# Chunk attention with two gated feed-forward layers on one Trainium2 core: when block 0's v, the first weights and block 1's q and k are issued

## The chip, the cores and the metric

One core of a Trainium2 chip runs the whole program in one launch. The metric is device time in microseconds (us), lower is better. The kernel before takes 1098.87 us (median of 3 runs, 1097.88 to 1102.31).

## What is computed

```python
B, H, S, D = q.shape                        # 4, 8, 768, 64
chunk, left_ctx, right_ctx = (32, 16, 8)
for c in range(S // chunk):
    k_ctx = k[:, :, l_start:r_end]          # 16 tokens left, 32 own, 8 right
    k_full = np.concatenate([mem_k, k_ctx], axis=2)   # 8 memory keys ahead
    v_full = np.concatenate([mem_v, v_ctx], axis=2)
    scores = scale * np.matmul(q_c, k_full.transpose(0, 1, 3, 2))
    scores = scores - np.max(scores, axis=-1, keepdims=True)
    a = np.exp(scores)
    a = a / (np.sum(a, axis=-1, keepdims=True) + 1e-09)
    out[:, :, c_start:c_end] = np.matmul(a, v_full)
x = out.transpose(0, 2, 1, 3).reshape(B * S, H * D)    # 3072 x 512
h = x @ w_in                                           # 512 x 2048
sp = np.where(h > 20.0, h, np.log1p(np.exp(np.minimum(h, 20.0))))
x = (h * np.tanh(sp)) @ w_out                          # first layer
h = x @ w2_in
return (h * (1.0 / (1.0 + np.exp(-1.702 * h)))) @ w2_out   # second layer
```

q, k, v and the memory are float32, the four weights float64.

## The kernel before, in words

The 3072 tokens are worked in 8 blocks of 384 (TB), two to a batch entry. For each block the attention of its 8 heads comes first, then the first product of layer 1 in 16 chunks of 128 columns (`forward(j, f)`, line 1151, run for f = 0 to 15): chunk f of block 0 is called f0 to f15 here. Block 0 multiplies in plain float32, all later blocks in three products of split values. The attention of block j + 1 is spread among the chunks of block j. Everything behind layer 1's first product is the same before and after and takes no part here.

**Block 0's attention** has 4 pairs of heads, each cut in two: 8 quads (`quad` and `quad_out`, lines 832 and 912). `first_pair` (line 760) loads q and k of a pair in one transfer each (192 KB and 208 KB, k of the first pair 200 KB; they are called q0 to q3 and k0 to k3), q from ACT and k from SP, and PE turns them (line 780). A quad then goes through scores on PE (line 848), masked minima on DVE (862), four exps on ACT (877), reciprocals and scaling (824 to 904, on DVE or ACT), turning on PE (923), a copy to SBUF (929, 930), the product with v (940) and a copy to x (975, 977). `first_memory` (line 739) loads block 0's memory keys and turns them (747). `first_values` (line 723) loads block 0's v for all heads from POOL: four transfers of 208 or 240 KB and four of 16 KB of memory values. A copy of one element on POOL (line 1115) reads the last of the four large ones; POOL's transfers of block 1's v stand behind that copy.

**Weights.** `w_conv` (line 403) loads a chunk of the first weight as float64 words, 512 KB from SP (these loads are W0 to W15), and turns the words to float32 in four steps: a scaled copy on ACT (line 423) or DVE, then a shift, an or and a sign on DVE (432, 436, 440). W8 to W15 go to tiles that hold block 0's raw and turned q and k until then. A conversion is paced by `begun`: the load of chunk f waits for the start of an earlier conversion (AHEAD = 6 back).

**Block 1's attention** goes in pairs of pairs (`pair_of_heads` and `duo`, lines 647 and 991): q and k of a pair come in 4 transfers each of 48 and 52 KB, with 128 bytes in a row, from SP; DVE turns them (679, 682). A duo's scores are 96 small products on PE (line 1003). The first duo's 16 transfers and the second duo's 16 stand on SP with W2 to W7 between them, and W8 follows the second.

**What sets the order.** Each operation is handed to a planner (`Plan`, line 135) with a rank, an engine and a cost; the planner sorts them into one order for each engine before the program is built, and each engine runs its list in that order. An engine that waits holds back all that stands behind it, also the issue of transfers. SP's transfers use 8 semaphores in turn (shared with ACT's), POOL's another 8: a transfer waits for the landing of the one eight before it.

Of the kernel before, what the change touches and what calls it, by code (L numbers as in the profile page):

```python
# [9 lines left out]
F32 = mybir.dt.float32  # L10
# [300 lines left out]
def kernel(  # L311
# [65 lines left out]
    def load(rank, buf, parts, nbytes, run, reads=(), via=0, on=None):  # L377

        for part in parts:
            def go(queue, part=part):  # L380
                o, i = part()
                queue.dma_start(out=o, in_=i)  # L382

            way = ("sp", 0.475, lambda go=go: go(nc.sync), bus(nbytes / len(parts), run))
            if via:
                way = ("pool", via, lambda go=go: go(nc.gpsimd), bus(nbytes / len(parts), run, True))
            if on == "act":
                way = ("act", 0.5, lambda go=go: go(nc.scalar), bus(nbytes / len(parts), run))
            add(rank, [way], reads=reads, writes=[buf])
# [3 lines left out]

    w_src = {
# [8 lines left out]
    def w_conv(layer, f, part, rank, after, v, st):  # L403
# [3 lines left out]
        pace_by = begun[-1 - AHEAD:-AHEAD] if (layer, part) == (1, 0) else [pace[rank - AHEADW]] if rank < L1 else []  # L407
# [195 lines left out]
    x0, mem_t, pace, started, opened = {}, {}, {}, [], []  # L603
# [43 lines left out]
    def pair_of_heads(j, hp, rank):  # L647
# [29 lines left out]
        load(rank - (LEAD if j == 1 and hp < 2 else 4), ql, qs, P * TB * 4, 128, passed(j, rank - AHEADK), via=NARROW * (j > 1))  # L677
        load(rank - (LEAD if j == 1 and hp < 2 else 4), kl, ks, P * NKB * 128, 128, passed(j, rank - AHEADK))
# [19 lines left out]
    def values_of(j, h0, rank):  # L698
# [21 lines left out]
        load(rank, vt, parts, P * NCH * D * 4, 256, opened if j == 1 else passed(j, rank - AHEADV), via=NARROW)  # L720
        return vt

    def first_values(gp, rank):
# [3 lines left out]
        for i in range(2):  # L727
            g = 2 * gp + i
            n0 = LEFT * (g == 0)
            load(rank, vt, [lambda i=i, g=g, n0=n0: (  # L730
                vt[n0:WIN, i], rows(v, g * GQ - LEFT + n0, [(1, WIN - n0), (S, H)], 0, D)
            )], WIN * H * D * 4, 256, via=WIDE)
        for i in range(2):
            load(rank + 0.1, vt, [lambda i=i: (
                vt[WIN:P, i], rows(mem_v, 0, [(1, NM), (NM, H)], 0, D)
            )], 0.05 * WIN * H * D * 4, 256, via=NARROW)
# [23 lines left out]
    def first_pair(hp, rank):  # L760
# [11 lines left out]
        )], 2 * TB * D * 4, 1024, on="act")  # L772
        load(rank - 4, kl, [lambda: (
# [311 lines left out]
    def quads():  # L1085

        last, todo = None, []
        for j in range(NB):
# [17 lines left out]
            for n in range(NQ):  # L1106
                rank = base + 2 * n
                if j == 0:
                    hp, gp = divmod(n, GB // 2)
                    if n == 0:  # L1110
                        first_memory(base - 6)
                        junk = sb.tile([P, 1], F32, name="junk")
# [5 lines left out]
                    if gp == 0:  # L1118
                        qT, kT, done = first_pair(hp, rank)
# [551 lines left out]
```

## Time and profile before

| | |
|---|---|
| median of 3 runs | 1098.87 us |
| the profiled execution | 1095.65 us |
| its span in the profile | 1093.9 us |
| PE, DVE, ACT, POOL busy | 98%, 73%, 49%, 15% of the span |
| DMA moved | 220.83 MB, 202 GB/s on average |
| granted clock of PE, mean of the span | 0.99 |

The profile is of one execution. The page gives busy times and costly groups for the whole span; windows, timelines and the DMA view give a stretch of it, with times in us from the start of the span. A timeline row merges like instructions that follow one another, and the bracket behind it gives the idle time of the engine ahead of it and what ended it. Each of PE's float32 products stands as two records. The granted clock is 1.00 at 2.4 GHz and 0.50 at 1.2 GHz.

### The profile page before, as it was taken

Reading aid. Unit: us, or ns where it says so; the run is one execution under the profiler, and the core shown is the slowest. Engines: PE = TensorE matmul, PEld = TensorE weight load, DVE = VectorE, ACT = ScalarE, POOL = GpSimd, SP = SyncE. Lnnn points to the kernel's source line nnn. Section 1 sums busy time; section 2 is a strip of 40 time slices with the busy share of each in tenths; the row PEclk is TensorE's granted clock in tenths of the full one; section 3 lists DMA queues with packets and bytes.
Section 4 is the critical chain, followed back from the end, with each engine's and each line's share of the span. In section 5 each row is a group of like instructions: output and inputs, shape, how many; then the busy total and the mean of one; then the engine's idle time right before and its main releaser. Section 6 shows DMA issues by size and latency. Waiting matters only on the chain.

```text
span 1093.9 us, 25367 instructions
## 1 busy us (share of the span) xinstructions
PE 1075.9 (98%) x9936; PEld 1039.9 (95%) x9936; DVE 799.5 (73%) x1430; ACT 539.3 (49%) x1209; POOL 163.9 (15%) x273
## 2 busy tenths in 40 slices
PE   6899999999999999999999999999999999999998
PEld 5568999999999999999999999999999999999998
DVE  4896566766677689889869867666657877877875
ACT  4763544544545354555454656565565533323332
POOL 5339347537500000000000000000000000000000
PEclk8799999999999999999999999999999999999999
DMA  9998989989988573573453776868678545355361
GB/s 182 225 249 214 256 256 265 211 244 275 251 268 277 182 233 117 181 245 123 160 173 100 223 251 226 297 216 291 217 256 268 155 121 160 107 146 139 103 167 46
DMA packets 238800, 220.83 MB, mean 202 GB/s; under 512 B 70105, under 2 KB 211997, under 8 KB 238681
## 3 DMA queue, kind: packets, MB, share of 16 engines
q1 hardware_dynamic: 227865, 202.22, 62.6%
q0 software_dynamic: 9984, 16.21, 6.8%
q8 instruction: 78, 1.28, 0.5%
q10 hardware_dynamic: 832, 0.79, 0.3%
q14 instruction: 41, 0.34, 0.1%
HBM read 137.85 MB, written 81.26 MB: 200 GB/s over the span
## 4 chain that ended last, share of the span: by engine, by line
PE 90%; DMA 5%; DVE 4%; issue 1%; ACT 0%; SPq 0%; DVEq 0%; ACTq 0%
PE o L1166 12%; PE h L1166 12%; PE h L1328 9%; PE o L1429 9%; PE o L1521 9%; PE o L1328 8%; PE h L1429 6%; PE s L1429 6%; PE h L1521 6%; PE s L1521 5%; PE s L1328 4%; PE s L1065 1%; DMA wo<-in_q_dram 1%; DMA wi<-in_moe_w_in_dram 1%; PE s L1003 1%
## 5 line engine op out<-in xcount | busy, mean ns | idle before, releaser
L1166 PE MATMUL h<-xh,wi 128*128 128x384 f32 x320 | 83.7, 343 | 0.0
L1166 PE MATMUL o<-xh,wi 128*128 128x384 f32 x320 | 82.8, 340 | 0.0
L1166 PEld LDWEIGHTS o<-xh,wi 128*128 128x128 f32 x320 | 57.1, 188 | 0.6
L1166 PEld LDWEIGHTS h<-xh,wi 128*128 128x128 f32 x320 | 56.9, 188 | 0.6
L1166 PE MATMUL h<-xl,wi 128*128 128x384 f32 x160 | 53.9, 337 | 0.0
L1166 PE MATMUL o<-xl,wi 128*128 128x384 f32 x160 | 53.8, 336 | 0.0
L382 POOL DMA_DIRECT2D vt<-in_v_dram x62 | 41.0, 666 | 30.8 <-PE o L940 14.0
L1298 ACT ACTIVATE e<-h 128x384 f32<-128x384 f32 (+2 forms) x47 | 22.4, 477 | 45.5 <-PE h L1521 28.5
L1511 DVE TENSOR_TENSOR xl<-vt,xh 128x1024 fp32r<-128x1024 f32 x24 | 29.4, 1223 | 20.1 <-ACT xh L1508 18.0
L1521 PE MATMUL o<-wo,xh 128*128 128x256 f32 x232 | 43.7, 282 | 0.0
L1511 DVE TENSOR_TENSOR xl<-wi,xh 128x1024 fp32r<-128x1024 f32 x32 | 38.8, 1221 | 6.6 <-ACT xh L1508 5.9
L1429 PE MATMUL o<-xh,wo 128*128 128x256 f32 x224 | 40.7, 282 | 0.0
L382 POOL DMA_DIRECT2D wo<-in_q_dram x48 | 30.4, 639 | 45.7 <-DMA g1d<-z 16.9
L382 POOL DMA_DIRECT2D wo<-in_v_dram x56 | 35.9, 646 | 5.4 <-DMA wo<-in_q_dram 2.1
L1412 DVE TENSOR_TENSOR xl<-z,xh 128x1024 fp32r<-128x1024 f32 x24 | 29.2, 1223 | 10.2 <-ACT xh L1408 9.4
L1166 PE MATMUL h<-wo,wi 128*128 128x384 f32 x192 | 36.2, 341 | 0.0
L1521 PEld LDWEIGHTS o<-wo,xh 128*128 128x128 f32 x232 | 35.8, 190 | 0.0
L1166 PE MATMUL o<-wo,wi 128*128 128x384 f32 x192 | 35.8, 340 | 0.0
L1508 ACT ACTIVATE xh<-wi 128x1024 fp32r<-128x1024 f32 x25 | 26.4, 1054 | 18.5 <-DMA wi<-gd 8.9
L1298 ACT ACTIVATE ev<-o 128x384 f32<-128x384 f32 (+2 forms) x31 | 14.6, 471 | 42.1 <-PE o L1521 17.9
L1429 PEld LDWEIGHTS o<-xh,wo 128*128 128x128 f32 x224 | 34.8, 191 | 0.0
L1025 ACT ACTIVATE e<-s,mx 128x64 f32<-128x64 f32 x84 | 25.1, 319 | 18.1 <-DVE mx L1020 18.1
(442 smaller groups left out, 3538.8 us busy)
## 6 DMA issues: line engine op xcount, KB each, us to landing
st<-in_moe_w_out_dram SPq DMA_DIRECT2D x32, 512.0 KB
st<-wd SPq DMA_DIRECT2D x29, 512.0 KB
z<-g1d SPq DMA_DIRECT2D x24, 512.0 KB
vt<-gd SPq DMA_DIRECT2D x24, 512.0 KB
wi<-gd SPq DMA_DIRECT2D x24, 512.0 KB
g1d<-gl SPq DMA_DIRECT2D x46, 192.0 KB
g1d<-z SPq DMA_DIRECT2D x45, 192.0 KB
wi<-in_moe_w_in_dram SPq DMA_DIRECT2D x16, 512.0 KB
```

The source lines that it names most:

```text
L382: queue.dma_start(out=o, in_=i)
L1003: nc.tensor.matmul(out=s[hh][c0:c0 + CHUNK, g, i], lhsT=qT[d, c * CHUNK:(c + 1) * CHUNK], rhs=keys[d, c * BLK:c * BLK + KEYS], start=True, ...
L1025: nc.scalar.activation(out=e[:, g, i], in_=s[hh][:, g, i], func=AF.Exp, scale=scale, bias=mx[:, g, i:i + 1], accum_out=sm[:, g, i:i + 1],)
L1065: nc.tensor.matmul(out=o[i][hh * D:(hh + 1) * D, cs], lhsT=vt[hh][d, c], rhs=aT[hh][d, cs], start=True, stop=True, tile_position=(i * D, h ...
L1166: nc.tensor.matmul(out=h.get(), lhsT=a[:, c], rhs=b.at(kk), start=(n == 0), stop=(n == KD * len(prods) - 1))
L1298: ("act", act(n, True), lambda: nc.scalar.activation(out=dst(), in_=bank.get(), func=AF.Copy)),
L1328: nc.tensor.matmul(out=bank.get(), lhsT=a, rhs=b, start=(fresh and m == 0), stop=(m == 3 * K2 - 1), skip_group_check=not fresh,)
L1412: add(rank + 0.05, [("dve", dve(n2), lambda gh=gh, gl=gl, src=src: nc.vector.tensor_tensor(out=flat(gl), in0=flat(src), in1=flat(gh), op=A ...
L1429: nc.tensor.matmul(out=bank[:, d, :], lhsT=a, rhs=b[:, p, :], start=(fresh and h == d == p == m == 0), stop=(h == 1 and p == HP - 1 and m ...
L1508: ("act", act(NP * P), lambda: nc.scalar.activation(out=flat(gh), in_=flat(src), func=AF.Copy)),
L1511: add(rank + 0.05, [("dve", dve(NP * P), lambda: nc.vector.tensor_tensor(out=flat(gl), in0=flat(src), in1=flat(gh), op=ALU.subtract))], re ...
L1521: nc.tensor.matmul(out=bank.get(), lhsT=a[:, p], rhs=b, start=(fresh and p == 0 and m == 0), stop=(p == NP - 1 and m == 2), skip_group_che ...
```

## The change

- POOL's transfers of block 0's v wait for k0: a new copy of one element on POOL reads k0, and v stands behind it.
- SP issues k0 first and the memory keys second.
- A new transfer of 4 bytes on SP, from the last of block 0's large v transfers to a tile `mark`, waits for that v. W0 and all that follows on SP (W1 to W15, block 1's q and k, stores) stands behind its issue; that it has landed is not waited for by W0.
- Block 1's v on POOL still stands behind the copy that reads the last large v.
- The planner's cost for block 0's v changes (the last argument of `bus`), and it sorts the lists of PE, ACT and DVE anew up to the end of block 0's chunks; from there the lists are the same.

```diff
@@ load
-                way = ("pool", via, lambda go=go: go(nc.gpsimd), bus(nbytes / len(parts), run, True))
+                way = ("pool", via, lambda go=go: go(nc.gpsimd), bus(nbytes / len(parts), run, rank > -12))
@@ ahead of w_conv
+    behind = []
@@ w_conv
-        pace_by = begun[-1 - AHEAD:-AHEAD] if (layer, part) == (1, 0) else [pace[rank - AHEADW]] if rank < L1 else []
+        pace_by = begun[-1 - AHEAD:-AHEAD] or behind if (layer, part) == (1, 0) else [pace[rank - AHEADW]] if rank < L1 else []
@@ pair_of_heads
-        load(rank - (LEAD if j == 1 and hp < 2 else 4), ql, qs, P * TB * 4, 128, passed(j, rank - AHEADK), via=NARROW * (j > 1))
-        load(rank - (LEAD if j == 1 and hp < 2 else 4), kl, ks, P * NKB * 128, 128, passed(j, rank - AHEADK))
+        load(rank - (LEAD if j == 1 and hp < 2 else 4), ql, qs, P * TB * 4, 128, behind if j == 1 else passed(j, rank - AHEADK), via=NARROW * (j > 1))
+        load(rank - (LEAD if j == 1 and hp < 2 else 4), kl, ks, P * NKB * 128, 128, behind if j == 1 else passed(j, rank - AHEADK))
@@ values_of
-        load(rank, vt, parts, P * NCH * D * 4, 256, opened if j == 1 else passed(j, rank - AHEADV), via=NARROW)
+        load(rank, vt, parts, P * NCH * D * 4, 256, opened[1:2] if j == 1 else passed(j, rank - AHEADV), via=NARROW)
@@ first_values
-            )], WIN * H * D * 4, 256, via=WIDE)
+            )], WIN * H * D * 4, 256, opened[:1], via=WIDE)
...
-            )], 0.05 * WIN * H * D * 4, 256, via=NARROW)
+            )], 0.05 * WIN * H * D * 4, 256, opened[:1], via=NARROW)
@@ first_pair
+        given.append((ql, kl))
@@ quads
-                        first_memory(base - 6)
-                        junk = sb.tile([P, 1], F32, name="junk")
+                        first_memory(base - 3.95)
+                        junk, mark = (sb.tile([P, 1], F32, name=x) for x in ("junk", "mark"))
+                        qT, kT, done = first_pair(0, rank)
+                        opened.append(fixed())
+                        add(base - 2, [("pool", 0.15, lambda: nc.gpsimd.tensor_copy(
+                            out=junk[32:33], in_=given[0][1][32:33, 0, 0, :1]
+                        ))], reads=[given[0][1]], writes=[opened[-1]])
                         vals0 = [first_values(i, base - 1 + 0.2 * i) for i in range(2)]
...
+                        behind.append(fixed())
+                        add(base + 0.5, [("sp", 0.475, lambda: nc.sync.dma_start(
+                            out=mark[:1], in_=vals0[1][:1, 1, 0, :1]
+                        ))], reads=[vals0[1]], writes=[behind[-1]])
-                    if gp == 0:
+                    elif gp == 0:
                         qT, kT, done = first_pair(hp, rank)
```

Where instructions moved, the lists of the two programs read as follows; what stands in brackets is the semaphore that an instruction waits for (DMAHW for transfers of SP and ACT, DMASW for POOL's).

SP, from its first transfer, before: `w` takes the memory keys, `wi_89` to `wi_113` k0 to k3, `wi_118` and `wi_120` W0 and W1, `wo_123` block 1's first q.

```order
L382 DMA w<-in_mem_k_dram 64x64
L382 DMA wi_89<-in_k_dram 100x2x256
L382 DMA wi_91<-in_k_dram 104x2x256
L382 DMA wi_109<-in_k_dram 104x2x256
L382 DMA wi_113<-in_k_dram 104x2x256 [waits DMAHW0_49]
L382 DMA wi_118<-in_moe_w_in_dram 128x4x256 [waits DMAHW1_49]
L382 DMA wi_120<-in_moe_w_in_dram 128x4x256 [waits DMAHW2_49]
L382 DMA wo_123<-in_q_dram 32x12x32 [waits DMAHW3_49]
```

SP in the changed kernel (`wi_88` is k0, `wi_336` and `wi_347` are W0 and W1):

```order
L382 DMA wi_88<-in_k_dram 100x2x256
L382 DMA w<-in_mem_k_dram 64x64
L382 DMA wi_91<-in_k_dram 104x2x256
L382 DMA wi_110<-in_k_dram 104x2x256
L382 DMA wi_113<-in_k_dram 104x2x256 [waits DMAHW0_49]
L1126 DMA mark<-vt 1x1 [waits DMAHW1_49,DMASW5_49]
L382 DMA wi_336<-in_moe_w_in_dram 128x4x256 [waits DMAHW2_49]
L382 DMA wi_347<-in_moe_w_in_dram 128x4x256 [waits DMAHW3_49]
L382 DMA wo_362<-in_q_dram 32x12x32 [waits DMAHW4_49]
```

k0 and the memory keys have changed places, and `mark`, which waits for POOL's sixth transfer, the last large v, stands ahead of W0.

ACT behind the exps of quad 0, before: the exps of quad 1 (`ev`), then the conversion of W0.

```order
L877 ACTIVATE ev,sm<-ev,mx 96x128 [waits DVE_49] x2
L877 ACTIVATE ev,sm<-ev,mx 96x128
L877 ACTIVATE ev,sm<-ev,mx 96x128 [waits DVE_49]
L423 ACTIVATE wo_291<-wi_118 128x512 [waits DMAHW1_49]
L877 ACTIVATE e,sm<-e,mx 96x128 [waits DVE_49] x2
L877 ACTIVATE e,sm<-e,mx 96x128
L877 ACTIVATE e,sm<-e,mx 96x128 [waits DVE_49]
L929 ACTIVATE z_325<-o_318 128x384 [waits PE_49]
```

ACT from the same place in the changed kernel; `wi_155` takes the turned k of pair 3 and `xh` the first part of x.

```order
L879 ACTIVATE ev,sm<-ev,mx 96x128 [waits DVE_49] x2
L879 ACTIVATE ev,sm<-ev,mx 96x128
L879 ACTIVATE ev,sm<-ev,mx 96x128 [waits DVE_49]
L906 ACTIVATE e<-e,r 96x128 [waits DVE_49,Activation_49]
L906 ACTIVATE e<-e,r 96x128 [waits Activation_49] x3
L879 ACTIVATE e,sm<-e,mx 96x128
L879 ACTIVATE e,sm<-e,mx 96x128 [waits DVE_49]
...
L879 ACTIVATE ev,sm<-ev,mx 96x128 [waits DVE_49]
L808 ACTIVATE wi_155<-h 128x120 [waits DVE_49,PE_49]
L808 ACTIVATE wi_155<-h 128x120
L977 ACTIVATE xh<-o_326 128x192 [waits PE_49]
```

The conversion of W0 is no longer on ACT, where the exps of quad 2 stood behind it; a scaling of quad 0 stands in its place. Between these rows and f0 ACT has no conversion; two splits of W0 and W1 stand among the last quads.

PE at f0, before (`wo_422` and `wo_505` are the turned k of block 1's first duo; 96 scores run from the third row here):

```order
L923 MATMUL o_525<-ident,ev 128x96 [waits DVE_49,PE_49]
L923 MATMUL o_525<-ident,ev 128x96 x3
L1003 MATMUL s_534<-wo_422 32x64 [waits Pool_49]
L1003 MATMUL o_536<-wo_422 32x64
...
L1003 MATMUL o_536<-wo_505 32x64
L940 MATMUL o_593<-z_325,vt 64x96 [waits DVE_49]
...
L940 MATMUL o_662<-z_325,vt 64x96 [waits DVE_49]
L940 MATMUL o_662<-z_325,vt 64x96 x3
L1166 MATMUL h<-xh,wo_291 128x384 x3
L1166 MATMUL h<-xh,wo_291 128x384 [waits DVE_49]
```

PE at the same place in the changed kernel (`wo_527` and `wo_577` are the turned k, `wo_480` holds W0 and W1):

```order
L942 MATMUL o_583<-z_303,vt 64x96 [waits Activation_49]
L942 MATMUL o_583<-z_303,vt 64x96 x3
L1177 MATMUL h<-xh,wo_480 128x384 x3
L1177 MATMUL h<-xh,wo_480 128x384 [waits Activation_49]
L1005 MATMUL s_617<-wo_527 32x64 [waits DVE_49]
L1005 MATMUL o_619<-wo_527 32x64
...
L1005 MATMUL o_619<-wo_577 32x64
L1177 MATMUL h<-xh,wo_480 128x384 x4
L1177 MATMUL o_701<-xh,wo_609 128x384 [waits DVE_49,PE_49]
```

The duo's 96 scores, which stood ahead of the products with v of the last three quads, now stand between f0 (the first two rows of line 1177) and f1 (the last but one).

## Rows read from the trace of the kernel before

**Rows 1.** The page's first part: TensorE's busy time, share, instructions.

```profile
PE 1075.9 (98%) x9936; PEld 1039.9 (95%) x9936; DVE 799.5 (73%) x1430; ACT 539.3 (49%) x1209; POOL 163.9 (15%) x273
```

**Rows 2.** Windows: busy us (count) of PE, PEld, DVE, ACT, POOL; clock, DMA share, GB/s.

```profile
10.00:42.00 32.00, 22.81 (x337) 17.76 (x334) 24.56 (x123) 24.14 (x106) 9.54 (x17) 0.73 1.13 218
40.00:45.00 5.00, 4.35 (x17) 2.61 (x16) 4.55 (x15) 5.00 (x27) 4.75 (x8) 0.50 1.11 151
42.00:54.00 12.00, 12.00 (x38) 7.14 (x37) 9.46 (x23) 7.11 (x23) 8.09 (x16) 0.86 1.19 171
54.00:72.00 18.00, 17.30 (x239) 10.67 (x238) 17.52 (x40) 12.18 (x40) 3.64 (x6) 1.00 1.04 279
```

**Rows 3.** Timeline of PE: start us, us, engine, line, operation, tiles, count, [idle before, releaser].

```profile
22.14 0.91 PE L940 MATMUL o<-z,vt 128*64 128x96 f32 x8 [4.16 <-POOL wo L686]
...
34.80 0.24 PE L1003 MATMUL s<-wo 64*32 64x64 f32 x1
...
36.22 0.91 PE L940 MATMUL o<-z,vt 128*64 128x96 f32 x8
...
42.00 4.47 PE L1166 MATMUL h<-xh,wo 128*128 128x384 f32 x8
...
46.63 2.75 PE L1166 MATMUL h<-xh,wo 128*128 128x384 f32 x8
...
71.56 0.52 PE L1045 MATMUL s<-ident,e 128*128 128x128 f32 x3 [0.70 <-DVE e L1037]
```

**Rows 4.** Timeline of POOL: block 0's v, and the copy that waits for it.

```profile
2.19 2.08 POOL L382 DMA_DIRECT2D vt<-in_v_dram  x2
...
5.39 1.85 POOL L382 DMA_DIRECT2D vt<-in_v_dram  x2
...
18.01 0.18 POOL L1115 COPY junk<-vt 1x1 f32<-1x1 f32 x1 [9.63 <-DMA vt<-in_v_dram]
```

**Rows 5.** Timeline of ACT, 11 to 29 us and at 55 us.

```profile
11.04 0.40 ACT L877 ACTIVATE e<-e,mx 96x128 f32<-96x128 f32 x1 [0.74 <-DVE mx L862]
...
19.46 0.66 ACT L423 ACTIVATE wo<-wi 128x512 f32<-128x512 f32 x1 [5.20 <-DMA wi<-in_moe_w_in_dram]
20.03 0.39 ACT L877 ACTIVATE e<-e,mx 96x128 f32<-96x128 f32 x1
...
21.56 0.47 ACT L929 ACTIVATE z<-o 128x384 f32<-128x384 f32 x1
...
25.70 1.28 ACT L904 ACTIVATE ev<-ev,r 96x128 f32<-96x128 f32 x4 [1.05 <-DVE r L827]
...
28.63 0.33 ACT L975 ACTIVATE xh<-o 128x192 f32<-128x192 f32 x1 [0.87 <-PE o L940]
...
55.26 0.70 ACT L423 ACTIVATE wo<-wi 128x512 f32<-128x512 f32 x1 [3.21 <-DMA wi<-in_moe_w_in_dram]
```

**Rows 6.** Timeline of SP's queue: issues of W and of block 1's q.

```profile
3.97 2.98 SPq L382 DMA_DIRECT2D wi<-in_moe_w_in_dram  x2
6.99 11.70 SPq L382 DMA_DIRECT2D wo<-in_q_dram  x4
...
28.56 5.68 SPq L382 DMA_DIRECT2D wi<-in_moe_w_in_dram  x6
...
48.84 6.51 SPq L382 DMA_DIRECT2D wi<-in_moe_w_in_dram  x6
```

**Rows 7.** DMA view, 0 to 18 us, last row 18 to 34: KB, median us to landing.

```profile
DMA packets 3185, 3.42 MB, mean 190 GB/s; under 512 B 632, under 2 KB 2920, under 8 KB 3184
...
vt<-in_v_dram POOLq DMA_DIRECT2D x3, 240.0 KB, 10.7
...
wo<-in_v_dram POOLq DMA_DIRECT2D x4, 96.0 KB, 5.7
```

**Rows 8.** Timeline of DVE at block 1's last k.

```profile
54.00 0.61 DVE L682 STREAM_TRANSPOSE wo<-z 128x416 f32<-128x416 f32 x1 [1.69 <-DMA z<-in_k_dram]
...
56.48 1.28 DVE L440 SCALAR_TENSOR_TENSOR wo<-wi,wo 128x512 int32<-128x512 int32 x2
```

More of the change, by code (lines that the diff above doesn't have):

```diff
@@ L601, in rows @@
         )
-    x0, mem_t, pace, started, opened = {}, {}, {}, [], []
+    x0, mem_t, pace, started, opened, given = {}, {}, {}, [], [], []
     class Inputs:
```

## The prediction

> **What bounds the kernel now.** First the busy time by engine: TensorE (PE) is busy for 1075.9 of 1093.9 us [rows 1], so at most 18 us of idling and some slow clock can be won. The windows say where it lies. From 10 to 42 us PE is busy for 22.81 of 32 us at a mean granted clock of 0.73; from 42 to 54 it is busy throughout; from 54 to 72 it lacks 0.70 [rows 2]. From there it does not stop, so the prize is the date at which the chunk products f0 to f15 of block 0 begin: 42.00 us [rows 3].
>
> The PE timeline shows the gap ahead of it: the values product of quad 0 starts at 22.14 after 4.16 us of idling [rows 3]. v is not the whole cause. The last of its four large transfers is there at 18.01 [rows 4], but the ACT timeline shows the other one: after the exps of quads 0 and 1, ACT's next instruction is the conversion of W0, for which it waits 5.20 us, until 19.46; the exps of quad 2 stand behind it (20.03) and the copy that feeds the first values product behind those (21.56) [rows 5]. W0 was issued in the stretch that starts at 3.97 [rows 6]: it was in flight for some 15 us, beside q, k and v.
>
> **The change part by part.** *v and W.* In the first 18 us 3.42 MB moved [rows 7]. Block 0 needs 4x192 + 200 + 3x208 KB of q and k, 208 + 3x240 of v, 64 of memory values and 16 of memory keys, 2600 KB or 2.66 MB (the shapes of the transfers). The other 0.76 MB was W and block 1's q. Held back, at 3.42 MB in some 16 us of moving (0.21 MB/us), they give 3.6 us: v at 14.4. Against that v starts later: k0 now goes first on SP, 0.65 us sooner, without memory keys ahead and v beside it. In the trace it was there at about 6.5, when SP's second W was let through (3.97 + 2.98 less its own issue) [rows 6]; I take 5.6. POOL needs 4.1 us from the first to the fourth large v (2.19 to 5.39 + half of 1.85) [rows 4], and v then lands between 5.7 us (the smaller v of block 1) and 10.7 us (v in the crowd) after its issue [rows 7]: 15.4 to 20.4. I take 15.4, nearest to the lower row since the crowd is what is taken away.
>
> *The front, to f0.* ACT no longer meets W0: DVE converts W0 and W1 after the last quads' minima. ACT's list from the first exp to the last copy that f0 needs is 8 quads of 4 exps at 1.53 (20.03 to 21.56), 3 scalings at 1.28, one pair of small copies of k (0.4, about a copy of x), 7 copies of x at 0.33, 5 copies of turned weights at 0.47 and 2 splits of W, for which the nearest row is a conversion at 0.66 [rows 5]: 12.2 + 3.8 + 0.4 + 2.3 + 2.4 + 1.3 = 22.4 us. The first exp began at 11.04 [rows 5]; with k0 earlier, 10.5. Without a pause ACT is done at 32.9. In the trace it also paused for 1.05 and 0.87 us beside the W wait [rows 5]: 34.9 with those. The worst end is all of its idling from 10 to 42 (32 less 24.14 = 7.9 us [rows 2]): 40.8. I take **34.9, so f0 starts 7.1 us sooner** (1.2 to 9.1). DVE, busy for 24.56 of those 32 us [rows 2], has room for the same move. v at 15.4 costs nothing here: by ACT's list the first copy of x comes at 10.5 + 4x1.53 + 1.28 + 0.43 = 18.3, and the values product is wanted just ahead of that. This cover is gone if v lands after about 18.
>
> *Moved behind f0.* The scores of block 1's first duo, 96 small products from 34.80 to 36.22 [rows 3], stand after f0 now: **+1.4 us** once PE is full.
>
> *The hole behind v.* SP waits with mark, W0, W1, 16 transfers of block 1's q and k, W2 to W7, the second 16 and W8 queued behind it. In the trace the first 16 are through when W2 is issued, at 28.56, and W8 goes at 48.84 [rows 6]; ACT gets W8 at 55.26 after a wait of 3.21 [rows 5]. After the change the 16 start at about 17 instead of 6.99, but there they spent 11.70 us on four issues [rows 6], caught behind W, k and v. As 12 of them took 28.56 - 18.69 = 9.9 us, 16 take 13 us: they end at 30, 1.5 us later than before. So W8 comes at 56.8, and f8 can start after ACT's conversion (0.7) and three operations on DVE of up to 0.64 [rows 8], some 3 us with what is queued between them: 60.5. Before, f8 is what PE ends at 70.86, ahead of the 0.70 of idling; at 2.75 us like f1 [rows 3] it began at 68.1, and 5.7 us sooner is 62.4. Covered, with 2 us to spare: **0**. On this wait the Trainium skill has a rule: "DMA: Bandwidth & Descriptors", section "Anatomy of one DMA — SWDGE (gpsimd) path", gives each transfer about 2.0 us of fixed cost, most of it the receipt of the last write, so a queue that is started on a landing stands dry that long. By that page W8 would be at 57.3 and the sum unchanged; no row here shows a dry queue, since the DMA share is 1.13 over those 32 us [rows 2].
>
> *The 4-byte transfer, the memory keys second, POOL's small copy.* SP's mark is one more issue, about 0.5 us, inside the 1.5. Memory keys behind k0 are first wanted when PE's warm-up ends; at worst they delay what I took for k0 by 0.5 us. POOL's copy is 0.18 us [rows 4]. All under cover: 0.
>
> **Sum:** -7.1 + 1.4 = **-5.7 us**. Against the profiled execution, 1095.65 us, that is 1089.95. The median of the runs is 3.2 us above that execution, 1098.87, so the predicted time is **1093.2 us**.
>
> **The rivals.** *DMA takes back half.* DMA is over 1.0 busy from 10 to 72 us [rows 2], DVE already waited 1.69 us at 54.00 for block 1's last k [rows 8], and all bytes are still to be moved. If the 16 end 5 us later than before instead of 1.5, W8 is there at 60.3, f8 at 64.0 to 65.6 instead of 62.4, and PE stands 1.6 to 3.2 us: 1093.2 + 2.4 = 1095.6. For it: the start 10 us later. Against: the cover of 2 us, and the trace's 16 spent most of their time held up by what is now gone. Chance 0.25.
>
> *ACT runs through and the clock holds.* Without the two pauses f0 starts 2 us sooner. f0 took 4.47 us, f1 2.75 [rows 3], because PE had the lower level, 1.2 GHz, from 40 to 45 us (granted 0.50 [rows 2]). A PE that is busier ahead of f0 could keep 2.4 GHz: another 1.7. Together 1093.2 - 3.7 = 1089.5. Against: the mean clock from 10 to 42 is 0.73 although PE worked for 22.81 us of it [rows 2]. Chance 0.15.
>
> *v does not come sooner: the change doesn't do what it says.* v's own queue may be what takes 11 us, so that starting it 3 us later lands it at 18 or after. Against: 0.76 MB fewer ahead of it. Then the first copy of x waits from 18.3 to about 19, W0 and all behind it come another 2.6 us later and the cover of f8 is used up by 0.6: 1093.2 + 1.3 = 1094.5. The Trainium skill speaks for this in "DMA: Bandwidth & Descriptors", section "Issuing engines are not separate DMA queues": transfers of all issuers run on the same 16 DMA engines and interleave, and another issuer saves only issue time. By that rule alone the order of issue would not bring v forward. Rows 7 go against it here as far as bytes go, since what is not yet issued cannot interleave. Chance 0.13.
>
> *Slower: block 1's q and k come late and PE waits behind f0.* PE takes instructions in order, and the duo's 96 scores now stand between f0 and f1. If the 16 transfers need as long as in the trace from the first on, 28.5 - 6.99 = 21.5 us, they end at 38.5, land 5 us later, and f1 starts near 46.6, as before; W8 then comes at 65.3, f8 at 69 to 70 instead of 68.1; with v at 18 each of these is 2.6 us worse: +1 to +5 us, 1099.9 to 1104. It decides from the point where W8 lands after 64, which is 8.5 us later than before. For it: their pace in the trace. Against: most of that was waiting for W and for v's crowd. Chance 0.06.
>
> **How the numbers follow.** 0.41 for the forecast; the rivals have 0.25, 0.15, 0.13 and 0.06. About 0.5%, 5.5 us, is what a measurement of this kernel can tell from no change; the bound is at 1093.4, next to the forecast. Faster by more: half of the forecast's 0.41, all of the clock's case and a few hundredths of the others, 0.42. Slower by more: only the last rival's upper half and noise, 0.05. Within: 0.53. The range runs from 1088.5, just past the case of a held clock, to 1098.0, past the cases of half a gain, with most of the last rival left out.
>
> **What would show it.** Right: no ACT wait for W of several us before 20 us; v there at 14 to 17; first values product at 16 to 19; f0 at 33 to 37; W2 issued near 30; W8 converted at 56 to 59 with PE never waiting for it; PE idle ahead of 42 us several us less. Wrong: f0 early and then gaps at the duo's scores, at f2 or at f6 to f8 (DMA took it back); v at 18 or later; f0 later than 38.

## The result, and the profile after

| | before | after |
|---|---|---|
| median | 1098.61 us (11 runs, 1095.96 to 1102.31) | **1105.24 us** (11 runs, 1103.72 to 1113.79) |
| profiled execution, its span | 1095.65, 1093.9 us | 1107.53, 1105.7 us |

The ratio is 1.0074, with a 95% interval of 1.0057 to 1.0090: **slower by 0.7%**. The forecast was 1093.2 us, 12 us less.

The busy time says little: PE worked 1078.7 us where it had 1075.9 [rows 1]; what grew is its idling. The windows of after say where (columns as in [rows 2]):

```profile
10.00:42.00 32.00, 23.42 (x343) 17.14 (x340) 25.79 (x123) 23.53 (x97) 15.24 (x26) 0.84 0.93 175
40.00:45.00 5.00, 5.00 (x109) 3.37 (x109) 3.02 (x10) 4.41 (x19) 1.93 (x4) 1.00 1.13 211
42.00:54.00 12.00, 10.58 (x37) 6.06 (x35) 7.88 (x22) 6.83 (x30) 2.07 (x3) 1.00 1.05 190
54.00:72.00 18.00, 13.98 (x225) 8.32 (x224) 14.24 (x30) 8.17 (x24) 10.44 (x19) 1.00 0.91 225
66.00:90.00 24.00, 17.61 (x138) 10.35 (x139) 18.71 (x44) 13.20 (x42) 9.11 (x15) 0.86 0.95 224
14.00:16.00 2.00, 1.92 (x38) 1.60 (x34) 2.00 (x17) 1.88 (x8) 0.00 (x0) 1.00 0.46 91
16.00:18.00 2.00, 2.00 (x29) 1.58 (x29) 2.00 (x13) 2.00 (x12) 0.56 (x2) 1.00 0.03 7
```

Up to 45 us PE is better off than in [rows 2]: 23.42 of 32 us, and full from 40 to 45. Then it loses 1.42 us from 42 to 54, 4.02 from 54 to 72, and 6.39 from 66 to 90, at a mean clock of 0.86; the last two windows overlap, and before each of them lost 0.70. The last two rows show a stretch that the trace of before does not have: from 14 to 18 us the transfers nearly stop. The same windows before:

```profile
14.00:16.00 2.00, 0.94 (x20) 0.69 (x16) 2.00 (x17) 0.27 (x2) 0.00 (x0) 1.00 1.12 210
16.00:18.00 2.00, 1.41 (x20) 1.13 (x20) 0.90 (x5) 0.00 (x0) 0.00 (x0) 1.00 1.04 192
```

PE's timeline of after, from the first values product on (columns as in [rows 3]):

```profile
17.04 0.55 PE L942 MATMUL o<-z,vt 128*64 128x96 f32 x8
...
31.32 0.88 PE L925 MATMUL o<-ident,e 96*128 96x96 f32 x4 [3.21 <-DVE r L826]
...
35.94 4.21 PE L1177 MATMUL h<-xh,wo 128*128 128x384 f32 x8
...
50.63 0.52 PE L1047 MATMUL s<-ident,e 128*128 128x128 f32 x3 [1.42 <-DVE r L826]
...
54.86 2.85 PE L1177 MATMUL h<-xh,wo 128*128 128x384 f32 x8 [0.80 <-DVE wo L441]
...
66.83 2.82 PE L1177 MATMUL h<-xh,wo 128*128 128x384 f32 x8 [0.87 <-DVE wo L441]
72.25 4.54 PE L1177 MATMUL h<-xh,wo 128*128 128x384 f32 x8 [2.60 <-DVE wo L441]
...
87.84 8.44 PE L1177 MATMUL h<-xh,wo 128*128 128x384 f32 x16 [2.25 <-ACT z L1309]
...
102.37 0.81 PE L1177 MATMUL h<-xh,wi 128*128 128x384 f32 x2
```

The first values product starts at 17.04 instead of 22.14 [rows 3], and f0 at 35.94 instead of 42.00: 6.06 us won. The rows at 66.83 and 72.25 are f8 and f9; both wait for a chunk of W to be turned to float32 (DVE line 441 is the last step of that), and behind their waits f9 and the pair at 87.84 run for the most part at the lower clock level, 1.2 GHz: 4.54 us for 8 records against 2.75 (granted clock 0.62 from 72.25 to 76.80), 8.44 for 16 against 5.43 (0.67 from 87.84 to 96.10). The last row is the first product of block 1, called **b1** from here. Before, the last pair and b1 stood at:

```profile
88.07 5.43 PE L1166 MATMUL o<-xh,wo 128*128 128x384 f32 x16
93.04 0.81 PE L1166 MATMUL h<-xh,wi 128*128 128x384 f32 x2
```

So b1 comes at 102.37 in place of 93.04, 9.3 us later, and f0 to b1 takes 66.43 us, before 51.04. From b1 on the lists are those of before. There the profiles of all the runs below take 1000 to 1007 us, in no order with what was changed, so a profiled execution tells where time went ahead of b1, and the median tells what it is worth: 6.6 us here.

SP's queue and ACT's conversions of W (columns as in [rows 6] and [rows 5]):

```profile
17.34 0.68 SPq L1126 DMA_DIRECT2D mark<-vt  x1
18.07 0.96 SPq L382 DMA_DIRECT2D wi<-in_moe_w_in_dram  x2
19.07 2.80 SPq L382 DMA_DIRECT2D wo<-in_q_dram  x4
...
33.22 4.19 SPq L382 DMA_DIRECT2D wi<-in_moe_w_in_dram  x6
37.51 10.57 SPq L382 DMA_DIRECT2D wo<-in_q_dram  x4
48.18 4.89 SPq L382 DMA_DIRECT2D wo<-in_k_dram  x4
...
57.30 0.41 SPq L382 DMA_DIRECT2D wi<-in_moe_w_in_dram  x1
57.80 1.26 SPq L382 DMA_DIRECT2D g1d<-z  x1
59.15 1.06 SPq L382 DMA_DIRECT2D wi<-in_moe_w_in_dram  x2
```

```profile
49.51 0.67 ACT L424 ACTIVATE wo<-wi 128x512 f32<-128x512 f32 x1 [2.97 <-DMA wi<-in_moe_w_in_dram]
...
62.72 0.70 ACT L424 ACTIVATE wo<-wi 128x512 f32<-128x512 f32 x1 [0.30 <-DMA wi<-in_moe_w_in_dram]
66.36 0.66 ACT L424 ACTIVATE wo<-wi 128x512 f32<-128x512 f32 x1 [2.49 <-DMA wi<-in_moe_w_in_dram]
...
86.37 0.66 ACT L424 ACTIVATE wo<-wi 128x512 f32<-128x512 f32 x1 [2.10 <-DMA wi<-in_moe_w_in_dram]
```

W2 goes at 33.22 (28.56 before [rows 6]), W8 at 57.30 (48.84). W8 is converted at 62.72, 7.5 us later than in [rows 5], and W9 to W13 follow 2.9 to 3.6 us apart. Two things moved: SP starts later, and from W2 to W8 it needs 24.1 us instead of 20.3. The second has its trace in POOL's timeline. Block 1's v goes in two sets of 0.8 MB, in 256-byte rows. The first follows the junk copy; the **second v set** goes to the tile that held block 0's v (vt), and waits until PE has read that. First the kernel before, then after:

```profile
40.25 1.28 POOL L382 DMA_DIRECT2D vt<-in_v_dram  x2 [14.03 <-PE o L940]
```

```profile
17.38 0.17 POOL L1122 COPY junk<-vt 1x1 f32<-1x1 f32 x1 [5.29 <-DMA vt<-in_v_dram]
...
34.27 1.28 POOL L382 DMA_DIRECT2D vt<-in_v_dram  x2 [6.31 <-PE o L925]
```

Block 0's v is free 6 us sooner because the front is faster, so the set starts 6 us sooner, and lies beside W2 to W7 instead of beside the second 16 transfers.

### The profile page after: what moved, and what is told of

Same layout as the page of the kernel before. It is cut to its first block, busy times and chain, and to the rows that moved or that the text cites. A ratio compares the mean times of both kernels' runs of the same rounds, so it can differ in the third digit from the quotient of the medians.

```text
span 1105.7 us, 25387 instructions
## 1 busy us (share of the span) xinstructions
PE 1078.7 (98%) x9936; PEld 1039.0 (94%) x9936; DVE 800.0 (72%) x1427; ACT 540.5 (49%) x1213; POOL 163.0 (15%) x273
## 4 chain that ended last, share of the span: by engine, by line
PE 87%; DMA 7%; DVE 2%; SPq 2%; issue 1%; ACT 1%; POOL 0%; DVEq 0%; ACTq 0%; POOLq 0%
PE h L1177 12%; PE o L1177 11%; PE o L1532 9%; PE o L1440 9%; PE h L1339 8%; PE o L1339 7%; PE h L1532 6%; PE h L1440 6%; PE s L1532 6%; PE s L1440 6%; PE s L1339 4%; DMA wi<-in_moe_w_in_dram 2%; SPq L382 2%; PE s L1067 1%; DMA wi<-gd 1%; DMA g1d<-gl 1%
## 5 line engine op out<-in xcount | busy, mean ns | idle before, releaser
L1423 DVE TENSOR_TENSOR xl<-z,xh 128x1024 fp32r<-128x1024 f32 x24 | 29.2, 1223 | 10.4 <-ACT xh L1419 9.4
L1177 PE MATMUL h<-xh,wo 128*128 128x384 f32 x64 | 28.3, 597 | 6.6 <-DVE wo L441 4.3
```

The source lines that it names most:

```text
L1177: nc.tensor.matmul(out=h.get(), lhsT=a[:, c], rhs=b.at(kk), start=(n == 0), stop=(n == KD * len(prods) - 1))
L1423: add(rank + 0.05, [("dve", dve(n2), lambda gh=gh, gl=gl, src=src: nc.vector.tensor_tensor(out=flat(gl), in0=flat(src), in1=flat(gh), op=A ...
```

## The experiments

All runs in one table, of 4 to 12 executions each. "Lists" says whether the engines' orders are those of the kernel before (old) or of the change (new), and "SP's hold" whose landing SP's mark waits for. f0, b1 and "set", the second v set, are starts, W2 and W8 are issues on SP; these columns are in us, of the profiled execution. Ratios are to the kernel before run beside them. Its median went from 1097.89 to 1099.25 over the five groups of runs (e1 to e4, e5 to e7, e8 to e10, e11 and e12, e13 and e14), so from group to group the ratios are the better guide.

| label | lists | SP's hold | f0 | W2 | W8 | set | b1 | median | ratio (95%) |
|---|---|---|---|---|---|---|---|---|---|
| before | old | none | 42.00 | 28.56 | 48.84 | 40.25 | 93.04 | 1098.61 | |
| after | new | v | 35.94 | 33.22 | 57.30 | 34.27 | 102.37 | 1105.24 | 1.0074 (1.0057 to 1.0090) |
| e1_no_hold | new | none | 36.61 | 27.21 | 52.03 | 34.95 | 94.97 | 1100.32 | 1.0028 (1.0013 to 1.0042) |
| e2_old_lists_hold | old | v | 44.47 | 31.98 | 51.74 | 42.90 | 95.62 | 1100.88 | 1.0026 (1.0010 to 1.0042) |
| e3_hold_k3 | new | k3 | 34.62 | 28.15 | 50.95 | 32.96 | 92.88 | 1100.91 | 1.0023 (1.0005 to 1.0041) |
| e4_v_at_once | new | v | 34.69 | 32.87 | 58.35 | 33.02 | 104.10 | 1105.26 | 1.0064 (1.0043 to 1.0084) |
| e5_no_hold_w14_sooner | new | none | 36.83 | 26.90 | 53.11 | 35.16 | 100.07 | 1103.10 | 1.0046 (1.0028 to 1.0064) |
| e6_hold_w14_sooner | new | v | 36.13 | 32.90 | 57.48 | 34.46 | 105.72 | 1108.77 | 1.0093 (1.0063 to 1.0124) |
| e7_no_hold_w_in_row | new | none | 38.46 | 27.62 | 53.48 | 36.79 | 105.34 | 1109.00 | 1.0090 (1.0056 to 1.0123) |
| e8_no_hold_cut | new | none | 37.48 | 26.04 | 49.84 | 35.81 | 91.27 | 1096.98 | 0.9984 (0.9970 to 0.9998) |
| e9_before_cut | old | none | 41.59 | 28.55 | 46.34 | 39.84 | 92.15 | 1097.28 | 0.9984 (0.9971 to 0.9998) |
| e10_hold_cut | new | v | 35.92 | 32.70 | 55.26 | 34.26 | 100.61 | 1104.99 | 1.0051 (1.0035 to 1.0067) |
| e11_no_hold_v2_late | new | none | 37.79 | 25.80 | 51.54 | 41.08 | 92.37 | 1096.61 | 0.9980 (0.9963 to 0.9996) |
| e12_hold_v2_late | new | v | 35.53 | 32.64 | 52.79 | 42.27 | 95.22 | 1100.05 | 1.0015 (0.9995 to 1.0036) |
| e13_hold_k3_v2_late | new | k3 | 34.66 | 27.47 | 49.07 | 37.84 | 89.51 | **1094.01** | **0.9948** (0.9930 to 0.9966) |
| e14_no_hold_v2_later | new | none | 36.69 | 27.52 | 48.65 | 44.01 | 92.74 | 1096.77 | 0.9978 (0.9965 to 0.9990) |

The time follows b1, not f0: the four runs with b1 above 101, and e5 and e10 at 100, have the six longest medians, whatever f0 is. (The profiles of e1 and e3 are of the shortest of their ten executions, 1097.52 and 1095.18; there the median is the better guide.)

**The hold and the lists, apart.** The first four runs take the change's parts singly. e1 issues nothing where the mark was:

```diff
-add(base + 0.5, [("sp", 0.475, lambda: nc.sync.dma_start(out=mark[:1], in_=vals0[1][:1, 1, 0, :1]))], ...
+add(base + 0.5, [("sp", 0.475, lambda: None)], ...
```

> The changed kernel's lists on every engine, without the 4-byte transfer: W0 and all that follows goes out on SP as soon as its semaphores let it. Hold theory (the wait on SP is the cost: a dry stretch of DMA behind v, then W2 to W8 and block 1's q and k late): f0 still starts at 36 to 38 us, v lands near 18, W2 goes out near 28.5 and W8 near 49 instead of 33.2 and 57.3; 1092 to 1096 us, some 10 us less than the changed kernel. Lists theory (the re-sorted lists, with the duo's scores behind f0, are the cost): W8 comes early but PE still stands at f2 to f8; 1103 to 1107 us. POOL theory (v behind k0 is the cost): 1101 to 1105 us.

e2 is the kernel before with the mark issued just ahead of W0, and with the operations of block 0's v moved ahead of it in the program (the cut shows the mark alone):

```diff
+                if layer == 1 and f == 0:
+                    nc.sync.dma_start(out=held0["mark"][:1], in_=held0["v"][:1, 1, 0, :1])
```

> The lists of the kernel before on every engine, v at once on POOL as there, with the 4-byte transfer put ahead of W0 on SP. Hold theory: ACT still meets W0 ahead of quad 2's exps, now at 20 to 22 us instead of 19.46, W8 goes out at 53 to 58 us: 1103 to 1110 us. Lists theory: as the kernel before within 2 us, 1097 to 1100.

e3 lets the mark read k3 in place of v, e4 takes POOL's wait for k0 away:

```diff
-    out=mark[:1], in_=vals0[1][:1, 1, 0, :1]
+    out=mark[32:33], in_=given[3][1][32:33, 0, 0, :1]
```

```diff
-add(base - 2, [("pool", 0.15, lambda: nc.gpsimd.tensor_copy(out=junk[32:33], in_=given[0][1][32:33, 0, 0, :1]))], ...
+add(base - 2, [("pool", 0.15, lambda: None)], ...
```

> The changed kernel's lists, with the 4-byte transfer reading k3 instead of the last large v, so that SP is let go when block 0's k is there, at 9 to 12 us instead of 17.3. Hold theory: no dry stretch of DMA behind v, W2 out at 28 to 31, W8 at 50 to 53: 1093 to 1098 us. Lists theory: 1103 to 1107.

> The changed kernel's lists with the hold on SP, without POOL's wait for k0: v is issued from 2.2 us on as before. Hold theory: v lands at 14 to 15.5 instead of 17.3, SP is let go as much sooner, and the time falls by about that: 1102 to 1104.5. POOL theory: v's late start is the cost, 1097 to 1100. Lists theory: 1103 to 1107.

Measured: 1100.32, 1100.88, 1100.91 and 1105.26. Neither part alone makes the loss: the new lists alone cost 0.28%, the hold alone 0.26%, both 0.74%; whether the two simply add up, the intervals do not tell. POOL's wait for k0 has no part in it: without it (e4) v lets SP go 1.0 us sooner, at 16.34, and the time stays. With the old lists the hold buys nothing: W0's conversion still stands ahead of quad 2's exps on ACT, and f0 comes at 44.47. With the new lists and no hold f0 is 5.4 us sooner and b1 still 1.9 us later than before. So something behind f0 takes the lead back even where SP is not held.

**A miss: the place of W14 and W15.** In e1, ACT waited for W14 at 80.30, and PE stood 2.35 us behind that. On SP the memory keys and block 1's next k had come ahead of W14 and W15. e5 and e6 move those two loads up, e7 all of W8 to W15:

```diff
+[order.insert(at(f - 1) + 1, order.pop(at(f))) for f in (14, 15)]     # e7: range(9, 16)
```

> The new lists without the hold, as in the first experiment, and on SP the loads of W14 and W15 moved up, from behind the memory keys and block 1's next k (issued at 75.7 and 76.8 us there) to right behind W13. In the first experiment ACT waited 1.66 us for W14 at 80.30 with a copy out of PSUM behind it, PE waited 2.35 us for that copy at 79.4, and the pair of products behind the gap ran at half clock for 1.7 us more (7.12 us for 16 records, 5.43 before). Theory: this place of W14 and W15 on SP is what the new lists lose; then the waits at 79 to 82 go, the first product of block 1 starts 3 to 5 us sooner than the 94.97 of the first experiment, and the time is 1095 to 1097.5 us, at or under the kernel before. Rival: the lists lose by the stores of g1d between W8 and W13 and by the second v set that was moved up; then PE waits elsewhere at 66 to 90 us and the time stays at 1099.5 to 1101.

> The change as it is, hold included, with W14 and W15 moved up on SP to right behind W13. Theory: the change loses by two things that add: the place of W14 and W15 (2.25 us of PE's wait at 87.84 and 3.0 us of half clock behind it, 8.44 for 5.43) and the hold's lateness for W2 to W13 (PE's waits for W's words at 54 to 72 us, 4.3 us in all, and 1.8 us of half clock). With the first taken away the time falls by 3 to 5 us, to 1100 to 1102, and stays above the kernel before. Rival: the hold alone sets the end, W14 and W15 are late for the same reason as the rest; then it stays at 1104 to 1106.

> The new lists without the hold, and on SP all of W8 to W15 in a row, ahead of the stores of g1d. If the stores between the loads cost nothing on their own, this equals the one that moves W14 and W15 alone, within 1 us. If they do, it is 1 to 3 us less. Against both: the stores wait behind eight loads, and the buffers that they free come late; then ACT waits for g1d and the time is above that one by 1 to 3 us.

None is faster than its parent, where e5 and e6 were expected to be 3 to 5 us faster: by the ratios e5 and e6 are 0.2% slower, which is within the intervals, and e7 0.6%, which is not. b1 comes 5.1, 3.4 and 10.4 us later. The waits of PE and ACT in e5 (us in total, times, longest), and then its SP queue, say why:

```profile
PE o L1175 <- ACT gl L1307: 6.2, 1, 6.2
...
ACT gl L1307 <- DMA g1d<-gl: 4.3, 1, 4.3
```

```profile
57.76 8.33 SPq L382 DMA_DIRECT2D wi<-in_moe_w_in_dram  x4
66.19 2.59 SPq L382 DMA_DIRECT2D g1d<-gl  x1
```

The four loads hold SP for 8.33 us and land 16.0 us after their issue at the median. The store behind them frees the tile that ACT copies the next chunk into, and ACT starts that copy only at 78.95; PE waits 6.2 us for the result space that the copy empties. The place that the planner had found for W14 and W15 was no worse: the theory fell.

**Is it the bytes? A cut.** The DMA engines are over 1.0 busy in e1 from 18 to 48 us (shares of 1.03 to 1.27 in stretches of 6 us; 0.72 from 48 to 54, which the expectation of e8 misses), as they are before [rows 2]. e8, e9 and e10 take 0.8 MB out just behind W7, by loading one run of 32 rows for each of the second 16 transfers in place of 12 or 13 (block 1's heads 4 to 7 are then computed from what stood in the tiles):

```diff
-parts = [(0, 32, 0, NKB, -LEFT)]
+parts = [(0, 32, 0, 1 if j == 1 and hp in (2, 3) else NKB, -LEFT)]      # and q alike
```

> The new lists without the hold, with every list as in the first experiment, but the second 16 transfers of block 1's q and k bring one run of 32 rows each in place of 12 or 13 (0.8 MB less in rows of 128 bytes; the rest of those two tiles is not loaded, so block 1's heads 4 to 7 are computed from what stood there). Theory of the DMA engines: from 18 to 72 us their busy share is 1.0 to 1.3 both before and in the first experiment, so f0's lead of 5.4 us cannot bring W8 to W15 any sooner. With 6 to 8 us of DMA time taken out of 35 to 52 us, W8 is issued at 44 to 47 us in place of 52.0, the lead is kept in part, block 1's first product starts at 88 to 91 us and the time is 1091 to 1095 us, below the same cut in the kernel before by 2 us or more. Rival: the new lists lose by their order alone (stores between the loads, W14 and W15 behind the memory keys); then the cut gains under 1.5 us and the time is 1098.5 to 1101.

> The kernel before with the same cut of 0.8 MB and nothing else (same heads computed from what stood there). PE is busy from 42 to 90 us there but for 0.7 us, so an emptier DMA has nothing to give: 1096.5 to 1098.5 by the theory of the DMA engines, no more than 1.5 us under the kernel before. By the rival the same. A fall of 3 us or more would say that the kernel before, too, was held by the transfers.

> The change as it is, hold included, with the same cut of 0.8 MB. Theory of the DMA engines: the hold costs 4 to 5 us of dry engines at 15 to 19.5 us, which nothing gives back while the engines are full; with 6 to 8 us taken out behind it, W8 comes at 49 to 51 us in place of 57.3, PE's waits for W's words at 54 to 72 us go, and the time is 1096 to 1100. Rival: SP's order and its stores set it; then it stays at 1103 or more.

By the ratios the cut gives 0.44% without the hold (1096.98 us), where the new lists then just draw level with the kernel before under the same cut, 0.16% in the kernel before (1097.28 us), and 0.23% with the hold (1104.99 us), which is within the intervals. The 1091 to 1095 us of e8 and the 1096 to 1100 of e10 did not come. So bytes are a part of the loss without the hold, and not what the hold costs. In e10 the 16 transfers, now of 4 KB, still hold SP from 37 to 55 us. SP's waits from 26 to 62 us (us in total, times, longest), then its queue:

```profile
SPq L382 <- DMA wi<-in_moe_w_in_dram: 9.9, 4, 3.9
```

```profile
37.03 3.17 SPq L382 DMA_DIRECT2D wo<-in_q_dram  x4
41.23 10.21 SPq L382 DMA_DIRECT2D wo<-in_k_dram  x4
```

SP waits 9.9 us for W2 to W7 to land before it may issue these, since it uses its eight semaphores in turn. So what W2 to W7 lie beside may be what sets W8; the next runs try that.

**The second v set held back.** e11, e12 and e13 are e1, the change and e3 with a copy of one word on POOL, ahead of the second v set, that waits until W5 has landed (`plan.stage`, filled elsewhere, keeps the tile of each W):

```diff
+if j == 1 and len(T["vh"].made) == 3:
+    late, first = sb.tile([P, 1], I32, name="late"), parts[0]
+    parts[0] = lambda: (nc.gpsimd.tensor_copy(out=late[:1], in_=plan.stage[5].get()[:1, :1]), first())[1]
```

> The new lists without the hold, as in the first experiment, and POOL waits for W5's landing (a copy of one word) ahead of the second v set, which it started at 34.95 us there, as soon as block 0's v was free, and at 40.25 in the kernel before. Theory: in the new lists this set (0.8 MB) goes beside W2 to W7 and keeps SP, which has eight transfers under way at most, from issuing the second 16 and W8 behind them: from W2's issue to W8's 24.8 us in the first experiment, 20.3 before. Held until W5 is there, the set goes beside the second 16, W2 to W8 takes 20 to 22 us, W8 is issued at 47 to 49.5, and the time falls by 2 to 4 us to 1096 to 1098.5. Rival: the issue of W8 depends on the first 16 and the W's alone, or the set then crowds W8 to W13; W8 stays at 51 or later and the time at 1099.5 to 1102.

> The change as it is, hold included, with the same wait ahead of the second v set (34.3 us there). Theory: W2 to W8 falls from 24.1 us to 20 to 22, W8 from 57.3 to 53.5 to 55, the time by 2 to 3 us to 1102 to 1103.5; what is left above the kernel before is the hold's own. Rival: no change, 1104.5 to 1106.

1096.61 and 1100.05: the set's place is worth 3.7 us without the hold and 5.2 with it by the medians, 0.48% and 0.59% by the ratios. The DMA view of 30 to 50 us (rates in 40 slices of 0.5 us, then size and median us to landing), first of after, then of e12:

```profile
GB/s 137 107 112 80 89 115 99 88 115 152 242 270 346 387 383 361 373 299 193 248 230 223 174 199 260 217 197 144 203 258 201 176 197 293 355 289 189 348 166 162
...
wi<-in_moe_w_in_dram SPq DMA_DIRECT2D x6, 512.0 KB, 12.9
vt<-in_v_dram POOLq DMA_DIRECT2D x4, 96.0 KB, 8.3
```

```profile
GB/s 97 109 114 99 99 105 92 126 164 279 281 352 383 383 363 363 352 354 354 356 350 350 367 344 354 340 248 260 197 146 128 136 145 185 141 181 142 152 139 99
...
wi<-in_moe_w_in_dram SPq DMA_DIRECT2D x6, 512.0 KB, 7.4
vt<-in_v_dram POOLq DMA_DIRECT2D x4, 96.0 KB, 5.5
```

Without the set beside them the rate is 344 to 383 GB/s from 35.5 to 42.5 us, and W2 to W7 land 7.4 us after their issue; with it the rate is between 144 and 299 from 38.5 to 46.5 us, and they land after 12.9. In e12 W8 is issued at 52.79 in place of 57.30. In e11 W8 moves by only 0.5 us, less than expected, though the time falls as expected: what shows there is W14, issued at 73.27 in place of 75.72 us, and PE's wait for the copy behind its conversion, 1.0 us in place of 2.35. From W2 to W8 it takes 25.7 us there, in e1 24.8, so without the hold the gain is measured, and its way through W8 is not shown.

> The change with the hold ended by k3 in place of v (the mark reads a word of k3, as in the third experiment, where it landed at 11.1 us), and POOL's wait for W5 ahead of the second v set. If what the change with the late set still loses against the one without the hold (1100.05 to 1096.61 us) is the stretch in which the transfers stand dry behind v, it goes with the shorter hold: 1095 to 1097.5, W2 at 27.5 to 29, W8 at 49 to 51. If any hold of W and of block 1's q and k costs, it is in between, 1098 to 1100.

> No hold, and the second v set waits for W7 in place of W5, so it starts at 45 to 47 us in place of 41.08. Theory: the set then goes beside the end of the second 16 and the start of W8 to W13; W8 is issued at 48 to 51 in place of 51.54, and what W8 to W13 lose to the set is about what W8 gains: 1095 to 1097.5, the same as with W5 within 1 us. Rival: any second v set beside W's costs what it cost beside W2 to W7, 1098 to 1100.

e13 gives **1094.01 us**, 0.5% below the kernel before and 11.2 us below the change; against e3 the set's place is worth 0.75%. e14 equals e11. So it matters that the set does not lie beside W2 to W7, and a still later place gains no more. And what the hold costs goes with the dry stretch, in which the transfers nearly stop: with the late set, no hold gives 1096.61, a hold to the landing of v 1100.05, a hold to the landing of k3 1094.01 (with the early set 1100.32, 1105.24 and 1100.91). That SP starts late is not the cost by itself: W0 goes 6.5 us later in e13 than in e11. The windows of e12 and then of e13 from 14 to 18 us:

```profile
14.00:16.00 2.00, 2.00 (x43) 1.72 (x40) 2.00 (x22) 1.85 (x9) 0.00 (x0) 1.00 0.37 74
16.00:18.00 2.00, 1.92 (x28) 1.55 (x28) 2.00 (x8) 2.00 (x12) 0.57 (x2) 1.00 0.02 5
```

```profile
14.00:16.00 2.00, 2.00 (x43) 1.72 (x39) 2.00 (x21) 1.85 (x9) 0.00 (x0) 1.00 1.00 183
16.00:18.00 2.00, 1.92 (x29) 1.55 (x28) 2.00 (x10) 2.00 (x12) 0.60 (x2) 1.00 1.09 310
```

In e13 POOL's junk copy sees v at 17.34, as early as with the full hold (17.37 in e12; 20.43 in e11 without one). W and block 1's q, issued from 12.02 on, do not delay v any more, and the transfers do not stop.

## Why the prediction was wrong

**What was right.** k0 was there in time for POOL's copy at 5.25 (5.6 taken). ACT meets no W0, and the first values product starts at 17.04 (16 to 19 said). f0 starts at 35.94; 34.9 was forecast, so the first term, -7.1, came out as -6.06. The longest pause of PE there, 3.21 us at 31.32, is not one that the forecast allowed for. PE waits for reciprocals on DVE, and ahead of these DVE stood still for block 1's first q, which the hold had kept back:

```profile
30.03 0.58 DVE L680 STREAM_TRANSPOSE wo<-wo 128x384 f32<-128x384 f32 x1 [1.86 <-DMA wo<-in_q_dram]
```

In e12 DVE waits 0.8 us there and f0 starts at 35.53; in e13, where q is issued 6 us sooner, DVE does not wait, and f0 starts at 34.66. So the hold cost some 1.3 us ahead of f0 too. The duo's 96 products stand behind f0, as said, and took 1.1 us of PE (1.4 taken). The held clock did not come: f0 took 4.21 us, at a granted clock of 0.66 from 36 to 40 us.

**v.** 15.4 was taken; the junk copy saw it at 17.38. The large transfers took 7.3 us at the median, inside the 5.7 to 10.7 of [rows 7]. The bytes held back were as forecast, 2.69 MB in the first 18 us (2.66 taken). Most of them were through sooner: in the DMA view of 0 to 18 us (rates in 40 slices of 0.45 us) the rate falls from 142 to 19 GB/s at 15.3 us.

```profile
GB/s 0 0 0 11 93 218 287 323 307 196 203 285 225 184 196 155 241 172 205 228 257 237 152 164 160 155 220 160 187 127 174 141 114 142 19 18 18 5 0 0
```

What still moves behind that, at 5 to 18 GB/s, is the tail of POOL's own queue, single packets, the last of them at 16.77 us; the copy goes 0.6 us later. So v came 2.0 us later than taken by a tail that the sum did not have. The whole dry stretch lasts 3.6 us, from 15.3 to 18.9: the tail 1.5, v's release 0.6, the mark's issue 0.7, and 0.9 from W0's issue at 18.07 until transfers run again.

The prediction cited the Trainium skill, "DMA: Bandwidth & Descriptors", section "Anatomy of one DMA — SWDGE (gpsimd) path": about 2.0 us of fixed cost per transfer, most of it the receipt of the last write. Behind v's last packet this trace shows 0.6 us, and the five other profiles with the full hold 0.6 to 1.0. The dry stretch that the prediction drew from the rule is there, and longer than 2.0 us; its consequence as the prediction put it, W8 0.5 us later, was too small.

**The step that failed: "The hole behind v", priced at 0.** It said that the 16 transfers start at 17, end at 30, that W8 then comes as long after W2 as before, at 56.8, and that f8, wanted at 62.4, is covered with 2 us to spare. Its parts:

- The start: v 2 us later than taken, then the mark and W0 and W1 ahead, so the first q goes at 19.07. The 16 need 14.2 us (13 taken). W2 goes at 33.22, 3.2 us later than the 30 that was taken. This cost is the hold's: 3.4 us of the time in e12 against e11.
- From W2 to W8, 20.3 us were carried over from [rows 6] as if nothing there changed. But the term that won 6 us at the front also let go of block 0's v 6 us sooner, and with it POOL's second v set, which went from beside the small transfers to beside W2 to W7: 24.1 us, and 5.2 us of the time (e12). This term was not in the sum at all. The text named the late part of the same queue, W8 behind the second 16, and asked only when SP would get there, not what POOL would put beside it. Nor did it ask when W2 to W7 themselves would land.
- So W8 was converted at 62.72, not 56.8, and f8 started at 66.83. But PE paused for W before that: the 1.42 us at 50.63, ahead of f4, are a wait for the duo's reciprocals, and ahead of these DVE had waited for one of W2 to W7:

```profile
47.79 0.43 DVE L427 TENSOR_SCALAR wo<-wi 128x512 f32<-128x512 f32 x1 [2.20 <-DMA wi<-in_moe_w_in_dram]
```

PE's waits from 50 to 90 us add up to 8.6 us (1.42 + 0.80 + 0.87 + 2.60 + 0.35 + 0.35 + 2.25), where before it had one of 0.70; the lower clock behind two of them cost 1.8 + 3.0, and the duo's products 1.1: 13.8 of the 15.4 us by which f0 to b1 grew. The rest is not assigned.

**The rivals.** "DMA takes back half" had the mechanism and 1095.6 us. Its condition, the 16 ending 5 us later than before, nearly came (33.22 for 28.56), but the set was missing in it too. "Slower" had the sign, with a chance of 0.06, and a wrong place: there is no gap at the duo's scores; the gaps are ahead of f4, f5, f8, f9, f11 and f12. Its point of decision, W8 landing after 64 us, was not reached either: W8 was converted at 62.72 and the loss was there. Of the signs that the prediction named for being wrong, the gap at f8 came. "v no sooner" was nearly true of v's landing, 17.38 after 18.01, and did not matter at the front: what the front had waited for was W0 on ACT. Behind it the lateness is part of the hold; that v let SP go 1.0 us sooner in e4 changed nothing.

**Right in the end, by another kernel.** With both costs cut down (e13) the time is 1094.01, next to the 1093.2 forecast for the change. That the two are so near is luck in part: in the profile of e13 f0 starts 7.3 us sooner than before and b1 3.5, where 5.7 was forecast. f0 to b1 still takes 3.8 us more than before, 1.1 of them the duo's products and 1.7 more idling of PE (2.36 us for 0.70). The gain at the front was real, and it reaches the end only as far as nothing behind f0 takes it back.

**Still open.** Why W2 to W7 and the set together move fewer bytes in a us than W alone is not settled; the runs show the rates only. Why the late set gains 3.7 us without the hold, where W8 hardly moves, is open too. Nor was it tried to start the set sooner in the kernel before, since block 0's v still stands in its tile.

## What to carry to other kernels

A stage that ends sooner frees its tiles sooner, and whatever transfer waits for such a tile starts then, beside other work than before. List, for each tile that the change frees earlier, the transfer that takes it and what lies beside that transfer at the new time. And a queue that is held until a landing can leave the DMA engines dry, here for 3.6 us; try to end the hold at an earlier event. Here that was the landing of k3, 6 us sooner: the engines stayed busy, and v landed as early.

## What the hardware showed

- While W2 to W7 (1024-byte rows) landed, the rate was 344 to 383 GB/s (e12, 35.5 to 42.5 us); with 0.8 MB of 256-byte rows on POOL's queue beside them it was 144 to 299 GB/s (after, 38.5 to 46.5 us). The DMA share does not show it: 1.08 in the first case (36 to 42 us of e12), 1.13 in the second (42 to 48 us of after).
- Transfers cut from 48 and 52 KB to 4 KB went hardly faster through SP (16 of them in 18.1 us in e10, 19.7 in after): the time of a queue whose issue waits for the landing of earlier transfers is not in its own bytes.
- A queue restarted on a landing left 3.6 us nearly without traffic (7 GB/s from 16 to 18 us of after). The release came 0.6 us behind the last packet of the queue it waited for, in the other profiles with the full hold 0.6 to 1.0.
